# Token layout and early issue order of a fused attention and feed-forward kernel: 64 lanes of 7 tokens against 112 lanes of 4, with another order of the first twelve pairs

## The chip, the cores and the metric

The kernel runs on one core of a Trainium2 chip. The core has five engines, each with its own instruction stream that is executed in order: TensorE (PE, matrix products), VectorE (DVE), ScalarE (ACT), GpSimd (POOL) and SyncE (SP, which here only issues DMAs). Engines wait for each other and for DMAs through semaphores. The metric is the device time of one execution in microseconds (us), where less is better. Several runs are made and their median is compared.

## The reference

```python
# q, k, v: 8 x 12 heads x 448 tokens x 64
q_n, k_n = rmsnorm(q, g_q), rmsnorm(k, g_k)      # x / sqrt(mean(x*x) + 1e-6) * g
scores = q_n @ k_n.T / sqrt(64)
attn   = softmax(scores)                         # + 1e-9 under the sum
x      = (attn @ v), heads side by side          # 3584 tokens x 768
h      = x @ w_in                                # 768 x 2048
out    = (h * sigmoid(1.702 * h)) @ w_out        # 2048 x 768
```

Attention with a root-mean-square norm on q and k is followed by a gated feed-forward layer over all tokens.

## The kernel before

**Tiling.** The unit of attention is a *pair*: two heads of one batch element. There are 48 pairs, six to a batch element. The 448 tokens of a pair are laid out on the partitions of on-chip memory. In the kernel before, a partition holds seven consecutive tokens and 64 lanes hold one head's tokens; q sits on the even partitions and k on the odd ones, so that the two share a tile of 128 partitions. v is loaded twice over the same way, four tokens on the even partition of a lane and four on the odd one, with the middle token in both.

**One pair.** `load` (L541 to L555) brings q, k and v in. `square` (L557) and `reduce` (L564) form the sums of squares. For the first six pairs `by_log` (L577) turns them into 1/rms with a logarithm and an exponential on ACT; later pairs are taken three at a time by `seed` and `rsqrt`, on DVE and POOL. `norm` (L614) scales the rows, on POOL mostly. The rows are then transposed so that the head dimension lies on the partitions: for the first twelve pairs by PE (`turn_pe`, with the copies `take_q` and `take_k` on DVE), for the others by a transposing DMA (`turn_dma`, with `scale_k` on ACT and `part_k` on POOL). `score` (L692) multiplies q and k, `expo` (L713) takes the exponential on ACT, and `values` (L731) multiplies with v, where a column of ones gives the softmax sums. `divide` (L748) divides by these, and the result is turned back into `xt`, the input of the feed-forward layer. `vcast` (L622) casts v to bf16.

With seven tokens a lane, keys are handled in three full chunks of 128 per head (two tokens each) and one chunk in which the last token of both heads shares the 128 partitions. `gG2`, `of_head` and `v_of_head` are the masks which that shared chunk needs: in `both_heads` on the key side, in `vcast` on the value side.

**Feed-forward.** `first` (L960), `tanh` (L970), `gate` (L982), then a second product: plain (L990) for the first part, afterwards in a Strassen form with sums on DVE (L1035) and products (L1044). PE's work here runs over all 128 partitions. The weights come in as eight DMAs issued by POOL (four quarters of `w_in`, L927, and four of `w_out`, L933).

**Buffers.** There are rings of seven raw q/k buffers, seven raw v buffers, six buffers of transposed q and k, and six of cast v. In the first part of the program some members of each ring are pieces of one large tile named `late`, which the feed-forward layer uses later: two of the seven raw q/k buffers, three of the raw v buffers, three of the transposed buffers and four of the cast v. A line of the profile with `late` as its tile is thus a load, a transposed operand or a cast v, according to its source line.

**What sets the order.** Every step is a task of an order that is written out when the program is built (`_Order`). A list scheduler with a duration for each task, and a model of two DMA queues, picks at each engine the ready task with the lowest key. The queues are the hardware queue that SP (and once ACT) feeds and the software queue that POOL feeds. When both have work, `share` says which part of full speed each gets. Keys of the first sixteen or so pairs' tasks come from a table (`KEYS`), earliest issue times of their loads and of the weights from another (`AT`), and a third (`ON`) names the tasks that run on their second choice of engine. PE gets small filler products (L529) where the scheduler leaves it idle. The engines then run this fixed order; waits on semaphores are put in for every tile that one instruction writes and another touches.

Of the kernel before, what the change touches and what calls it, by code (L numbers as in the profile page):

```python
# [26 lines left out]
class _Order:  # L27
# [36 lines left out]
    def run(self):  # L64
# [32 lines left out]
        def share(t):  # L97
            n = len(heads())
            if n != 2:
                return 1.0 / n  # L100
            return 0.65 if not queues["sw"] else 0.55 if t.eng == "POOL" else 0.5
# [124 lines left out]
    'g': -7.96, 'gT': -29.21, 'gG': -3.44, ('S', 0, 0): 20.14, ('R', 0, 0): 28.16, ('S', 0, 1):  # L226
    44.18, ('R', 0, 1): -37.1, ('Q', 0): 43.05, ('N', 0, 0): 37.04, ('N', 0, 1): 35.09, ('V',
    0): -24.15, ('T', 0, 0): -33.92, ('T', 0, 1): 14.65, ('KQ', 0): 28.15, ('K', 0): 55.2, ('S',
    1, 0): 8.44, ('R', 1, 0): 20.3, ('S', 1, 1): 40.54, ('R', 1, 1): 21.55, ('Q', 1): -38.14,
    ('N', 1, 0): 10.45, ('N', 1, 1): -15.44, ('V', 1): 15.95, ('T', 1, 0): 28.13, ('T', 1, 1):  # L230
    -33.93, ('KQ', 1): 50.88, ('K', 1): 48.8, ('S', 2, 0): 38.84, ('R', 2, 0): 8.79, ('Q', 2):
    13.62, ('N', 2, 0): 48.85, ('N', 2, 1): -24.39, ('V', 2): 40.55, ('T', 2, 0): -22.79, ('T',
    2, 1): -32.33, ('KQ', 2): 50.42, ('K', 2): -39.99, ('S', 3, 0): -4.3, ('R', 3, 0): 1.95,
    ('Q', 3): -34.1, ('N', 3, 0): -21.09, ('N', 3, 1): -3.62, ('V', 3): -4.91, ('T', 3, 0):
    -39.99, ('T', 3, 1): -18.9, ('KQ', 3): 50.91, ('K', 3): 46.36, ('S', 4, 0): 13.62, ('R', 4,
    0): 18.86, ('Q', 4): 36.65, ('N', 4, 0): -27.4, ('N', 4, 1): -14.52, ('V', 4): 8.33, ('T',
    4, 0): 60, ('T', 4, 1): -30.45, ('KQ', 4): 44.45, ('K', 4): 59.33, ('S', 5, 0): 15.52, ('R',
    5, 0): 50.42, ('Q', 5): 40.97, ('N', 5, 0): 51.99, ('N', 5, 1): 13.48, ('V', 5): 1.94, ('T',
    5, 0): -18.61, ('T', 5, 1): -29.22, ('KQ', 5): 28.16, ('K', 5): 1.08, ('L', 6, 0): -40,
    ('L', 6, 1): 14.08, ('L', 6, 2): -20.34, ('S', 6, 0): 10.24, ('R', 6, 0): -40, ('N', 6, 0):  # L240
    20.31, ('N', 6, 1): -15.44, ('V', 6): 8.34, ('T', 6, 0): -29.45, ('T', 6, 1): 15.28, ('KQ',
    6): 30.06, ('K', 6): -4.76, ('L', 7, 0): -31.18, ('L', 7, 1): 4.22, ('L', 7, 2): 57.6, ('S',
    7, 0): 32.32, ('R', 7, 0): 1.93, ('N', 7, 0): -7.89, ('N', 7, 1): -36.91, ('V', 7): 60,
    ('T', 7, 0): 5.3, ('T', 7, 1): -22.33, ('KQ', 7): 51.98, ('K', 7): 15.39, ('L', 8, 0):
    -14.16, ('L', 8, 1): -40, ('L', 8, 2): -20.32, ('S', 8, 0): 11.41, ('R', 8, 0): 59.33,
    ('Q0', 8): 53.43, ('Q', 8): -25.28, ('N', 8, 0): -3.63, ('N', 8, 1): -27.25, ('V', 8):
    28.31, ('T', 8, 0): 14.16, ('T', 8, 1): -40, ('KQ', 8): 1.15, ('K', 8): -8.89, ('L', 9, 0):
    -39.86, ('L', 9, 1): -11.5, ('L', 9, 2): 4.21, ('S', 9, 0): -14.54, ('R', 9, 0): 51.98,
    ('N', 9, 0): 35.63, ('N', 9, 1): -0.84, ('V', 9): 18.85, ('T', 9, 0): -23.2, ('T', 9, 1):
    -38.52, ('KQ', 9): 4.12, ('K', 9): 8.56, ('L', 10, 0): 12.98, ('L', 10, 1): 4.05, ('L', 10,  # L250
    2): -17.2, ('S', 10, 0): 10.46, ('R', 10, 0): 55.21, ('N', 10, 0): -7.97, ('N', 10, 1):
    0.16, ('V', 10): -24.2, ('T', 10, 0): -4.6, ('T', 10, 1): 9.68, ('KQ', 10): 8.78, ('K', 10):
    -3.43, ('L', 11, 0): -39.84, ('L', 11, 1): -39.67, ('L', 11, 2): 4.36, ('S', 11, 0): 42.54,
    ('R', 11, 0): -4.42, ('Q0', 11): -10.06, ('Q', 11): -14.57, ('N', 11, 0): 54.8, ('N', 11,
    1): 46.7, ('V', 11): 32.33, ('T', 11, 0): -39.99, ('T', 11, 1): -25.77, ('KQ', 11): 20.9,
    ('K', 11): 50.35, ('C', 0, 0, 0): -3.33, ('E', 0, 0, 0): 36.27, ('C', 0, 0, 1): -39.06,
    ('E', 0, 0, 1): 42.1, ('P', 0, 0, 0, 0): -18.92, ('P', 0, 0, 0, 1): -7.65, ('P', 0, 0, 0,
    2): -18.93, ('P', 0, 0, 0, 3): -39.99, ('O', 0, 0, 0): -40, ('B', 0, 0): -29.68, ('X', 0,
    0): 45.25, ('C', 1, 0, 0): 19.37, ('E', 1, 0, 0): -13.6, ('C', 1, 0, 1): -39.96, ('E', 1, 0,
    1): 13.61, ('P', 1, 0, 0, 0): -22.78, ('P', 1, 0, 0, 1): -40, ('P', 1, 0, 0, 2): -35.63,  # L260
    ('P', 1, 0, 0, 3): -35.79, ('O', 1, 0, 0): 1.36, ('B', 1, 0): 31.62, ('X', 1, 0): 50.63,
    ('C', 2, 0, 0): -18.6, ('E', 2, 0, 0): 13.51, ('C', 2, 0, 1): -25.35, ('E', 2, 0, 1): 51.3,
    ('P', 2, 0, 0, 0): -32.5, ('P', 2, 0, 0, 1): -39.99, ('P', 2, 0, 0, 2): -37.82, ('P', 2, 0,
    0, 3): -34.28, ('O', 2, 0, 0): 50.48, ('B', 2, 0): -39.07, ('X', 2, 0): 2.32, ('C', 3, 0,
    0): -29.04, ('E', 3, 0, 0): 8.46, ('C', 3, 0, 1): -29.48, ('E', 3, 0, 1): -22.67, ('P', 3,
    0, 0, 0): -20.87, ('P', 3, 0, 0, 1): -18.58, ('P', 3, 0, 0, 2): 15.26, ('P', 3, 0, 0, 3):
    -29.36, ('O', 3, 0, 0): 28.64, ('B', 3, 0): -35.53, ('X', 3, 0): -33.23, ('C', 4, 0, 0):
    -33.94, ('E', 4, 0, 0): -38.12, ('C', 4, 0, 1): -39.99, ('E', 4, 0, 1): 57.75, ('P', 4, 0,
    0, 0): -11.24, ('P', 4, 0, 0, 1): -40, ('P', 4, 0, 0, 2): -28.01, ('P', 4, 0, 0, 3): 15.27,
    ('O', 4, 0, 0): 50.21, ('B', 4, 0): -30.29, ('X', 4, 0): 8.79, ('C', 5, 0, 0): -19.24, ('E',  # L270
    5, 0, 0): -37.99, ('C', 5, 0, 1): -33.93, ('E', 5, 0, 1): 15.32, ('P', 5, 0, 0, 0): -32.06,
    ('P', 5, 0, 0, 1): 13.53, ('P', 5, 0, 0, 2): -18.89, ('P', 5, 0, 0, 3): 31.63, ('O', 5, 0,
    0): -0.32, ('B', 5, 0): -34.64, ('X', 5, 0): -8.9, ('C', 0, 1, 0): -25.97, ('E', 0, 1, 0):
    1.69, ('C', 0, 1, 1): -16.66, ('E', 0, 1, 1): 42.54, ('P', 0, 1, 0, 0): 20.38, ('P', 0, 1,
    0, 1): -35.54, ('P', 0, 1, 0, 2): -34.27, ('P', 0, 1, 0, 3): 18.62, ('O', 0, 1, 0): -0.33,
    ('B', 0, 1): -40, ('X', 0, 1): 59.93, ('C', 1, 1, 0): -40, ('E', 1, 1, 0): 59.1, ('C', 1, 1,
    1): -23.35, ('E', 1, 1, 1): 59.09, ('P', 1, 1, 0, 0): 19.56, ('P', 1, 1, 0, 1): -33.42,
    ('P', 1, 1, 0, 2): -23.22, ('P', 1, 1, 0, 3): 13.53, ('O', 1, 1, 0): 50.91, ('B', 1, 1):
    -31.11, ('X', 1, 1): -1.55, ('C', 2, 1, 0): -0.85, ('E', 2, 1, 0): -39.35, ('C', 2, 1, 1):
    13.53, ('E', 2, 1, 1): 12.93, ('P', 2, 1, 0, 0): 15.4, ('P', 2, 1, 0, 1): -0.36, ('P', 2, 1,  # L280
    0, 2): -33.43, ('P', 2, 1, 0, 3): 5.29, ('O', 2, 1, 0): 53.15, ('B', 2, 1): -39.05, ('X', 2,
    1): 32.15, ('C', 3, 1, 0): -20.21, ('E', 3, 1, 0): -0.21, ('C', 3, 1, 1): -34.68, ('E', 3,
    1, 1): -38.13, ('P', 3, 1, 0, 0): -4.54, ('P', 3, 1, 0, 1): -36.55, ('P', 3, 1, 0, 2):
    -0.32, ('P', 3, 1, 0, 3): 31.62, ('O', 3, 1, 0): 27.76, ('B', 3, 1): -40, ('X', 3, 1):
    28.15, ('C', 4, 1, 0): 9.08, ('E', 4, 1, 0): 42.53, ('C', 4, 1, 1): 4.27, ('E', 4, 1, 1):
    42.1, ('P', 4, 1, 0, 0): -4.29, ('P', 4, 1, 0, 1): 9.68, ('P', 4, 1, 0, 2): 9.81, ('P', 4,
    1, 0, 3): -28.0, ('O', 4, 1, 0): 50.2, ('B', 4, 1): -18.93, ('X', 4, 1): 13.19, ('C', 5, 1,
    0): -39.98, ('E', 5, 1, 0): -22.76, ('C', 5, 1, 1): -29.55, ('E', 5, 1, 1): 15.51, ('P', 5,
    1, 0, 0): -23.19, ('P', 5, 1, 0, 1): 4.26, ('P', 5, 1, 0, 2): -18.93, ('P', 5, 1, 0, 3):
    -35.21, ('O', 5, 1, 0): 8.55, ('B', 5, 1): 9.83, ('X', 5, 1): -40, ('C', 6, None, 0):  # L290
    -25.14, ('E', 6, None, 0): -22.75, ('E', 6, None, 1): 51.16, ('C', 6, None, 2): -40, ('E',
    6, None, 2): 13.49, ('E', 6, None, 3): 10.84, ('P', 6, None, 0, 0): -38.03, ('P', 6, None,
    0, 1): -30.29, ('P', 6, None, 0, 2): 41.42, ('P', 6, None, 0, 3): -34.28, ('O', 6, None, 0):
    58.71, ('P', 6, None, 1, 0): 24.43, ('P', 6, None, 1, 1): 3.72, ('P', 6, None, 1, 2):
    -32.51, ('P', 6, None, 1, 3): 13.54, ('O', 6, None, 1): -40, ('B', 6, None): -35.8, ('X', 6,
    None): 50.9, ('C', 7, None, 0): 18.62, ('E', 7, None, 0): 41.4, ('E', 7, None, 1): 33.89,
    ('C', 7, None, 2): 7.37, ('E', 7, None, 2): 60, ('E', 7, None, 3): 48.79, ('P', 7, None, 0,
# [1006 lines left out]
```

## Time and profile before

| | us |
|---|---|
| median of three runs (476.58 to 479.13) | 478.04 |
| the profiled execution | 478.04 |
| its span, first to last instruction | 476.3 |
| PE busy | 421.2 (88% of the span) |
| DVE / ACT / POOL busy | 295.3 / 280.3 / 203.5 |

The span is cut into 40 slices of 11.9 us by the page's second part, and the profile's table of windows gives the same for any stretch. Read so, the kernel has two parts. From about 97 us on PE is busy nearly without a break (43.00 us of the 43.00 from 97 to 140, 49.95 us of the 50.00 from 140 to 190). Before that it is busy 53.3 us of 97, and part of these are fillers. A busy share is an average, so an engine with half its time idle in the first part still tells nothing by itself: the chain of waits and the table of who waited for whom say what each idle stretch waited for. SPq and POOLq stand for the sequencers that issue DMAs. The bar of a DMA in the timeline is its issue; its data lands later.

### The profile page before, as it was taken

To read this page: it belongs to the slowest core of one execution; us is meant where nothing else is said; L and a number is where in the kernel's file an instruction comes from. 1 tells how busy PE (TensorE), PEld (TensorE's weight loads), DVE (VectorE), ACT (ScalarE), POOL (GpSimd) and SP (SyncE) were. 2 spreads that over 40 slices of the span, in tenths; PEclk is the share of its full clock that TensorE was granted. 3 is DMA by queue.
4 is the path that set the end of the run, shared out by engine and by line. 5 is a ranking of instruction groups with operands and counts; after the bars stand their busy time and mean duration, and the time that the engine had idled before them with its cause. 6 is when DMAs were issued, how large, how long until landed. Compare 5 with 4: busy or idle time off the path is not lost.

```text
span 476.3 us, 9605 instructions
## 1 busy us (share of the span) xinstructions
PE 421.2 (88%) x3604; PEld 250.1 (53%) x3604; DVE 295.3 (62%) x600; ACT 280.3 (59%) x431; POOL 203.5 (43%) x322
## 2 busy tenths in 40 slices
PE   4833388399999999998899999999999999999996
PEld 2422267287665555554455565445555555555563
DVE  3732257569769778658557874577666655565573
ACT  2541166177869886778479754696777456722410
POOL 5543237372673847726363773266464312000000
PEclk9756579789999999999899999999999999999999
DMA  5956669496377587676578567865653453013014
GB/s 171 244 153 146 128 128 209 132 189 168 65 186 138 112 203 173 166 193 146 133 183 205 121 145 179 179 171 134 158 126 79 105 128 81 19 28 77 0 43 108
DMA packets 94642, 64.93 MB, mean 136 GB/s; under 512 B 55684, under 2 KB 94596, under 8 KB 94596
## 3 DMA queue, kind: packets, MB, share of 16 engines
q1 hardware_dynamic: 86992, 57.60, 49.3%
q0 software_dynamic: 7296, 6.29, 8.7%
q8 instruction: 28, 0.46, 0.4%
q10 hardware_dynamic: 308, 0.43, 0.3%
q14 instruction: 18, 0.15, 0.1%
HBM read 47.19 MB, written 11.01 MB: 122 GB/s over the span
## 4 chain that ended last, share of the span: by engine, by line
PE 71%; DMA 10%; DVE 6%; issue 4%; SPq 3%; POOL 2%; ACT 2%; POOLq 0%; DVEq 0%; ACTq 0%
PE w L960 24%; PE w L1044 18%; PE o L744 6%; PE sc L707 6%; DMA late<-in_v_dram 4%; PE sc L1044 4%; PE w L990 3%; DMA raw<-in_k_dram 3%; PE o L741 3%; PE sc L710 3%; PE sc L960 2%; DVE late L1035 2%; SPq L548 2%; POOL row L619 1%; DVE ssq L571 1%
## 5 line engine op out<-in xcount | busy, mean ns | idle before, releaser
L719 ACT ACTIVATE att<-sc 128x896 bf16<-128x896 f32 (+1 forms) x168 | 130.2, 825 | 54.6 <-PE sc L707 54.2
L960 PE MATMUL w<-xt,w_in_s 128*128 128x448 bf16 (+1 forms) x810 | 152.4, 333 | 1.8 <-DVE g L982 1.8
L960 PEld LDWEIGHTS <-w_in_s 128*128 128x128 bf16 x864 | 80.1, 99 | 51.7 <-issue 3.3
L982 DVE SCALAR_TENSOR_TENSOR g<-th,w 128x448 bf16<-128x448 f32 x119 | 72.3, 616 | 26.4 <-ACT th L970 26.2
L970 ACT ACTIVATE th<-w 128x448 f32<-128x448 f32 x119 | 64.4, 548 | 34.3 <-PE w L960 32.0
L619 POOL TENSOR_TENSOR row<-raw,rs 128x384 bf16<-128x384 f32 (+1 forms) x85 | 84.2, 1011 | 0.9 <-issue 0.5
L626 POOL TENSOR_TENSOR vx<-vraw,v_of_head 128x512 bf16<-128x512 f32 x36 | 38.8, 1079 | 84.1 <-PE o L744 49.3
L744 PEld LDWEIGHTS <-att 128*128 128x128 bf16 x1152 | 63.7, 101 | 18.9 <-issue 2.8
L571 DVE TENSOR_REDUCE ssq<-sq 128x14 f32<-128x896 f32 (+1 forms) x50 | 51.9, 1043 | 27.0 <-ACT sq L562 26.2
L744 PE MATMUL o<-vx,att 128*128 128x65 bf16 x960 | 65.6, 196 | 0.0
L562 ACT ACTIVATE sq<-raw 128x896 f32<-128x896 f32 (+1 forms) x40 | 37.2, 933 | 23.8 <-DMA raw<-in_k_dram 13.4
L753 DVE RECIPROCAL rcp<-o 112x4 f32<-112x4 f32 x96 | 17.1, 178 | 48.7 <-PE o L744 48.4
L754 DVE TENSOR_TENSOR obs<-o,rcp 112x256 bf16<-112x256 f32 x96 | 40.8, 424 | 3.3
L707 PE MATMUL sc<-qk 64*128 64x448 bf16 (+1 forms) x270 | 41.7, 363 | 0.2 <-ACT att L719 0.2
L1044 PEld LDWEIGHTS <-late 128*128 128x128 bf16 x344 | 31.0, 98 | 19.9 <-issue 2.6
L741 PEld LDWEIGHTS <-att 128*128 128x128 bf16 x192 | 19.2, 100 | 41.8 <-issue 12.3
L1044 PEld LDWEIGHTS <-g 128*128 128x128 bf16 x336 | 30.4, 99 | 17.8 <-issue 1.5
L741 PE MATMUL o<-vx,att 128*128 128x130 bf16 x160 | 36.2, 226 | 4.0 <-DVE obs L754 3.3
L1044 PE MATMUL w<-w_out_s,g 128*128 128x384 bf16 x176 | 34.9, 335 | 0.0
L1044 PE MATMUL w<-w_out_s,late 128*128 128x384 bf16 x152 | 29.7, 326 | 0.3 <-DVE late L1035 0.2
L1044 PE MATMUL w<-late 128*128 128x384 bf16 x152 | 29.8, 327 | 0.0
L1057 DVE TENSOR_SCALAR osb<-w 128x384 f32<-128x384 f32 x29 | 16.2, 557 | 21.8 <-PE w L1044 21.7
(106 smaller groups left out, 469.7 us busy)
## 6 DMA issues: line engine op xcount, KB each, us to landing
vraw<-in_v_dram SPq DMA_DIRECT2D x84, 128.0 KB, 2.8
raw<-in_q_dram SPq DMA_DIRECT2D x44, 224.0 KB, 3.5
raw<-in_k_dram SPq DMA_DIRECT2D x43, 224.0 KB, 3.4
out_dram<-osb SPq DMA_DIRECT2D x88, 96.0 KB, 2.2
w_in_s<-in_moe_w_in_dram POOLq DMA_DIRECT2D x4, 768.0 KB, 9.6
w_out_s<-in_moe_w_out_dram POOLq DMA_DIRECT2D x4, 768.0 KB, 13.8
out_dram<-att SPq DMA_DIRECT2D x22, 96.0 KB, 2.2
late<-in_v_dram SPq DMA_DIRECT2D x12, 128.0 KB, 7.0
```

The source lines that it names most:

```text
L571: nc.vector.reduce_sum(out=ssq_of[g0][:, i - g0, part], in_=sq[i % N_SQ][:, part], axis=AX.X)
L619: eng.tensor_tensor(out=row_ring[i % N_QKN][:, gi:NT:2].rearrange("p n (h d) -> p h n d", h=2), in0=raw[turn(i, N_RAW, K_RAW)][:, :, ns], ...
L626: eng.tensor_tensor(out=vx_ring[turn(i, N_V, K_V)][:, :, :D], in0=vraw[turn(i, N_RAW, K_VRAW)][:, :, :], in1=v_of_head[:, :].to_broadcast( ...
L707: nc.tensor.matmul(sc[:, hp, lo:lo + n], lhsT=ks[r, c * WIN:(c + 1) * WIN], rhs=qs[r], start=True, stop=True)
L719: nc.scalar.activation(out=o, in_=sc[:, :, :S] if t < NC else sc[:, 0, :S], func=ACT.Exp)
L741: nc.tensor.matmul(o[:, x:x + 2, :], lhsT=att_of(u)[:, NT - 2, qs * SS:qs * SS + WIN], rhs=vx[:, NC:NC + 2, :], start=True, stop=True)
L744: nc.tensor.matmul(o[:, x, :], lhsT=att_of(u)[:, at, qs * SS:qs * SS + WIN], rhs=vx[:, (NC + 2) * hp + c, :], start=False, stop=(c == NC - 1),
L754: nc.vector.tensor_tensor(out=to[:SS, 2 * w:2 * w + 2].rearrange("p n h d -> p (n h) d"), in0=o[:SS, :, :D], in1=rcp[:SS, :].to_broadcast( ...
L960: nc.tensor.matmul(gps[b, m][:, j * SH:j * SH + n], lhsT=w_in_s[:, ki, f * 128:(f + 1) * 128], rhs=xT[b][:, ki, lo:lo + n], start=(ki == 0 ...
L970: nc.scalar.activation(out=th[:, :], in_=gps[b, m][:, :S], func=ACT.Tanh, scale=0.851)
L982: nc.vector.scalar_tensor_tensor(out=g_of[b // 2][:, f:f + len(g), lo:lo + n], in0=view(ths.pop((b, m))[:, :]), scalar=1.0, in1=view(gps.p ...
L1044: nc.tensor.matmul(held[to], lhsT=lhs[:, ko, :], rhs=y[:, ko, :], start=first and ko == 0, stop=ko == NK - 1, skip_group_check=not first)
```

## The change

The layout of tokens becomes 112 lanes of 4, with q and k side by side in the free dimension instead of on alternate partitions. A chunk of keys is then 112 tokens of one head, four chunks per head, and the shared chunk goes with its masks. v is loaded once, by one DMA. In the early transposes and the DMA transposes there are eight blocks of 112 in place of seven of 128. For the later pairs q is scaled by the gains instead of k, by one ACT instruction without the POOL one. Output rows are stored in pieces of up to 112 rows. On the side of the order, the shares in the scheduler's DMA model, the tables `KEYS`, `AT` and `ON` and the durations of many tasks are other ones. The number of PE's fillers is 78 in place of 77.

```diff
-            return 0.65 if not queues["sw"] else 0.55 if t.eng == "POOL" else 0.5
+            return 0.65 if not queues["sw"] else 0.69 if t.eng == "POOL" else 0.47
 KEYS = {
...
 AT = {
...
-    1): 12820, ('WI', 2): 4055, ('WI', 3): 32041, ('WO', 0): 27995, ('WO', 1): 6438, ('WO', 2):
-    20685, ('WO', 3): 53587}
+    15, 0): 18221, ('L', 15, 1): 27573, ('L', 15, 2): 45426, ('WI', 0): 11048, ('WI', 1): 3173,
+    ('WI', 2): 27789, ('WI', 3): 20304, ('WO', 0): 14524, ('WO', 1): 53302, ('WO', 2): 44189,
+    ('WO', 3): 21000}
...
-    late = consts.tile([128, 3 * T_LEN + N_SUM * S_LEN + 1056], BF16, name="late", tag="late")
+    late = consts.tile([128, 3 * T_LEN + N_SUM * S_LEN], BF16, name="late", tag="late")
...
-        src = (q, k, v)[which][b, h0:h0 + 2].rearrange("h (s n) d -> s h (n d)", n=NT)
+        src = (q, k, v)[which][b, h0:h0 + 2].rearrange("h (ss ns) d -> ss h ns d", ns=NS)
         if which == 2:
-            four = (NC + 1) * D
-            for side in range(2):
-                nc.sync.dma_start(
-                    out=vraw[turn(i, N_RAW, K_VRAW)][side::2].rearrange("p (h n) d -> p h (n d)", h=2),
-                    in_=bass.AP(tensor=src.tensor, offset=src.offset + side * four,
-                                ap=[[NT * D, LN], [S * D - D, 2], [1, four]]))
+            nc.sync.dma_start(out=vraw[turn(i, N_RAW, K_VRAW)][:SS], in_=src)
             return
         eng = nc.scalar if i == 0 and which == 1 else nc.sync
-        eng.dma_start(out=raw[turn(i, N_RAW, K_RAW)][which::2].rearrange("p h n d -> p h (n d)"),
-                      in_=src)
+        eng.dma_start(out=raw[turn(i, N_RAW, K_RAW)][:SS, which], in_=src)
...
-        nc.vector.tensor_scalar(
-            out=parts_of(i)[1].rearrange("p (c s e) -> p c e s", c=NC, e=2),
-            in0=lanes(x[:, :2 * NC * WIN])[:, 1], scalar1=gG[:, :], scalar2=None, op0=ALU.mult)
-        both_heads(i, nc.vector, x)
+        nc.vector.tensor_scalar(out=qk_ring[turn(i, N_KZ, K_KZ)][:, 1], in0=tps[i][:, 1],
+                                scalar1=gG[:, :], scalar2=None, op0=ALU.mult)
...
-    def scale_k(i):
-        nc.scalar.activation(out=parts_of(i)[1].rearrange("p (c s e) -> p c e s", c=NC, e=2),
-                             in_=lanes(turned(i)[:, :2 * NC * WIN])[:, 1], func=ACT.Identity,
-                             scale=gG[:, :])
-    def part_k(i):
-        both_heads(i, nc.gpsimd, turned(i))
+    def scale_q(i):
+        t = qk_ring[turn(i, N_KZ, K_KZ)][:, 0]
+        nc.scalar.activation(out=t, in_=t, func=ACT.Identity, scale=gG[:, :])
...
-        keys = [2 * c + hp for c in range(NC - 1)] + [NT - 3 + 2 * hp]
-        if hp == 0:
-            nc.tensor.matmul(o[:, x:x + 2, :], lhsT=att_of(u)[:, NT - 2, qs * SS:qs * SS + WIN],
-                             rhs=vx[:, NC:NC + 2, :], start=True, stop=True)
-        for c, at in enumerate(keys):
-            nc.tensor.matmul(o[:, x, :], lhsT=att_of(u)[:, at, qs * SS:qs * SS + WIN],
-                             rhs=vx[:, (NC + 2) * hp + c, :], start=False, stop=(c == NC - 1),
-                             skip_group_check=True)
+        for kc in range(NS):
+            nc.tensor.matmul(os_[u, w][:, x, :],
+                             lhsT=att_of(u)[:SS, kc, hp, qs * SS:qs * SS + WIN],
+                             rhs=vx_ring[turn(i, N_V, K_V)][:SS, hp, kc, :],
+                             start=(kc == 0), stop=(kc == NS - 1))
...
-            od.add(("KB", i), "POOL", 400, lambda i=i: part_k(i), at - 1.5,
-                   deps=[("T", i, 1), "gG"] + kz_free)
-            od.add(("KQ", i), "ACT", 625, lambda i=i: scale_k(i), at - 1.5,
+            od.add(("KQ", i), "ACT", 662, lambda i=i: scale_q(i), at - 1.5,
                    deps=[("T", i, 1), ("gG")])
...
-        for c in range(tm * 128, (tm + 1) * 128, LN):
-            b, n = 2 * bp + c // S, token_at[c % S // LN]
+        while c < (tm + 1) * 128:
+            b, j = 2 * bp + c // S, c % S
+            ns, ss = j // SS, j % SS
+            n = min(SS - ss, (tm + 1) * 128 - c)
```

## The prediction

> **What bounds the kernel now.** I first read the page's slices: the share of PE's time, the clock granted to it, and the DMA engines.
>
> ```profile
> PE   4833388399999999998899999999999999999996
> ...
> PEclk9756579789999999999899999999999999999999
> ...
> DMA  5956669496377587676578567865653453013014
> ```
>
> From the ninth slice on PE is full and its clock is up. Before that five slices show 3 or 4. The windows give the amounts (columns: start to end, length, then busy time of PE, PEld, DVE, ACT and POOL, each with its count, then the clock, the DMA share and GB/s):
>
> ```profile
> 14.00:97.00 83.00, 46.54 (x471) 32.34 (x471) 38.43 (x83) 32.37 (x48) 36.37 (x40) 0.71 0.71 158
> ...
> 140.00:190.00 50.00, 49.95 (x451) 28.25 (x450) 42.27 (x82) 41.06 (x64) 28.41 (x43) 1.00 0.73 160
> ```
>
> In the first no engine is even 60% busy, so something makes them all wait. The second is PE-bound; DVE (85%) and ACT (82%) come closest behind. PE's table of waits up to 97 us, its largest rows (total, times, longest):
>
> ```profile
> PE o L741 <- DMA late<-in_v_dram: 13.3, 3, 8.1
> PE w L637 <- POOL row L619: 9.0, 2, 8.1
> PE sc L707 <- DMA late<-in_v_dram: 7.9, 1, 7.9
> ...
> PE o L741 <- DMA late<-in_k_dram: 2.7, 1, 2.7
> PE sc L707 <- DMA late<-in_q_dram: 1.5, 1, 1.5
> ```
>
> These products read transposed q and k or cast v, yet wait for loads of raw tokens. The chain of waits (start, us, what) has the same loads on it:
>
> ```profile
> 20.89 7.59 DMA raw<-in_k_dram
> ...
> 39.18 7.03 DMA late<-in_v_dram
> ...
> 51.43 7.32 DMA late<-in_v_dram
> ```
>
> And this is the timeline of the second one, with all engines standing:
>
> ```profile
> 37.70 0.89 POOL L927 DMA_DIRECT2D w_in_s<-in_moe_w_in_dram  x1
> 38.52 1.25 SPq L548 DMA_DIRECT2D late<-in_v_dram  x2
> ...
> 46.30 0.69 DVE L626 TENSOR_TENSOR late<-late,v_of_head 128x512 bf16<-128x512 f32 x1 [7.92 <-DMA late<-in_v_dram]
> 46.34 0.56 PE L707 MATMUL sc<-late 64*128 64x224 bf16 x4 [7.89 <-DMA late<-in_v_dram]
> 46.37 2.15 POOL L560 TENSOR_TENSOR sq<-late 128x896 f32<-128x896 f32 x1 [7.79 <-DMA late<-in_v_dram]
> ```
>
> A load of v issued just after a quarter of `w_in` takes 7.0 us, where page part 6 has a median of 2.8 us for such loads. PE's scores and POOL's squares don't use its data and stand still all the same. The listing of the built programs, with each instruction's semaphores, says why: before, this product waits for two semaphores of v loads into `late`, and the earlier one on row 308 of PE for six DMAs. `late` is one tile with many pieces, and the waits treat a write on every second partition as touching all of it (why exactly is my reading). In the changed program PE's list has no wait for a load queue's semaphore up to its first operand from a transposing DMA, far into the full-PE part; ACT, DVE and POOL wait only for the loads that they read.
>
> **What the Trainium skill says.** "DMA: Bandwidth & Descriptors", section "Queues, rings and completion order": each DMA engine takes turns between queues, but drains a whole packet of descriptors (up to 64) before it switches. The trace agrees in kind: part 3 has 7296 packets on the software queue for eight weight loads, 912 each or 57 per engine, and a load behind one waited some 4 us longer than alone. The same page under "Why a DMA increments its semaphore by 16 and not by 1": the engines used are the largest number up to 16 that divides the outer dimension on both sides. 64 and 112 lanes and all new store pieces (16 to 112 rows) are multiples of 16, so no load falls to fewer engines; no run here shows it for 112. "TensorE: Matmul & The Clock Gate", "What's actually happening": an idle window of about 3.4 us drops PE's clock to half. The clock of 0.71 from 14 to 97 us agrees.
>
> **The change part by part**, against the profiled execution (span 476.3 us and 1.7 us around it, 478.04, which is also the median).
>
> 1. *Start.* SP's first load, which writes `late`, waited for POOL's memsets till 3.56 us; ACT issues its own load at 0.75. In the changed order SP's first load goes to `raw` and has no wait: 3.56 − 0.75 = 2.8 us less. Either end: 0 if the gains' load (read at 11.05) is what comes late, 3.5 at most. I take −2.8.
>
> 2. *False waits gone.* On PE: 13.3 + 7.9 + 2.7 + 1.5, and 8.1 of the row wait (ending 30.6), whose POOL instruction stood behind a cast into `late` waiting for the load of 20.89: together 33.5 us. On the chain: 7.59 + 7.03 + 7.32 and, further on, 2.94, 2.28, 2.87 and 3.57, 33.6 us. I take −33.5. The cover they gave goes too: loads and weights moved meanwhile.
>
> 3. *Weights come in clumps.* The changed POOL order has two quarters of `w_in` back to back behind its first square and two half norms, near 12 us (here the first norms end at 13 to 17), the other two behind a norm of pair 5, one of `w_out` a square later, and three of `w_out` together later. The software queue takes 8.7% of 476.3 us of all DMA engines, 41.4 us for eight, so 5.2 us each. The first clump holds the queue 10.4 us while loads of pairs 3 to 5 are still due (17 loads at SP's 0.605 us each take till 11 or 12 us to issue). These are true waits. They are covered in part by the attention of pairs 0 to 2; DVE and ACT stand behind them in order. From 0 to 10; I take +5. The second clump (15.6 us) meets the loads of pairs 7 and 8, whose sums of squares stand on DVE ahead of the first gates: 0 to 10, I take +4.
>
> 4. *DMA as a floor.* A pair was 224 + 224 + 256 KB; it becomes 3 x 224. At the second slice's 244 GB/s that is 3.0 and 2.8 us. Twelve pairs and eight weights: 34 + 41 = 75 us in place of 77. The second product needs its first `w_out` at 115 us now; 20 us earlier still leaves 95. No cost, but little slack.
>
> 5. *More vector work.* Squares, sums and norms go over 1024 elements in place of 896, on 112 partitions. Sum: 1080 x 1024/896 = 1.23 us, +0.15 on DVE for 48 pairs. Without stalls DVE has 38.4 + 2 us to do in some 60: +2.
>
> 6. *Late pairs on ACT.* Four exponentials of 896 in place of three and one of 448: 917 − 548 = +0.37. Square: 952 x 1024/896 = 1088, +0.14. Scaling 448 elements in one run instead of 384 in pieces (733): between −0.15 and +0.12, I take 0. So +0.5 us for 36 pairs, 18 us of ACT. PE covers it: in the densest window some six pairs add 3 us to ACT's 41 of 50 (and 1 to DVE's 42). Where cover fails, chains from load to exponential get longer; 0 to 12, I take +3. POOL loses `part_k` (0.45) and gains 0.2 on norms.
>
> 7. *PE.* `values` has 32 products of 65 columns in place of 28, four of which had 130. In the timeline the groups start 151.09, 151.34 and 151.59: 0.25 us for 7 with 520 columns, as many as in the new 8. If columns set it, nothing; if instructions, 1/7 more: 0.036 x 4 x 48 = 6.9 us. The product of 130 takes 0.06, the next six 0.19, so two of 65 against one of 130 are 0.063 to 0.060: 0.003 x 4 x 48 = 0.6. Transposes: one more in each of twelve pairs, 12 x 0.08 = 1.0. Scores: two rows of paired products take 0.5 us for 4, the shared chunk 0.22 alone: equal. +1.5.
>
> 8. *SP* issues three loads a pair for four; each has 224 rows for 128, so 0.6 to 1.06 us: −0.6 to +0.8 a pair, hidden since SP waits for buffers. Stores are as many as before. 0.
>
> Sum: −2.8 − 33.5 + 5 + 4 + 2 + 3 + 1.5 = −20.8, which gives 457.2 us.
>
> **The rivals.**
>
> *More is won.* Clumps hide behind work and the clock stays up: −36.3 + 1.5 and half of 5 and 6 (+2.5) is −32, 446; with a warm clock 440. For it: PE has only 46.5 us to do from 14 to 97, fillers included. Against: DMA share is 0.71 already.
>
> *Half is lost again.* True waits for clumped weights take 20 us in place of 9: 468.
>
> *Slower: starvation for the length of every clump.* A load behind one weight load took 7.0 to 7.6 us. At 7.3 each, clumps of two, three and three are 15, 22 and 22 us. If all engines stand in order behind a starved load each time, 59 us come in for 36 that go: 478 − 36 + 59 + 6 = 507; from about 30 us of it on, half, the kernel is slower. For: the engines' orders are fixed, and this trace shows what one late load does. Against: raw buffers for seven pairs are filled ahead, and in the changed program a late load stops only its readers.
>
> *It doesn't do what it says.* The named waits go from the listing, but the loads were due there anyway: same, 478. Against: the products that stood here at 39 and 51 us wait for no load in the changed listing.
>
> **How the numbers follow.** Forecast (448 to 466) 0.55; more won 0.17; half lost 0.12; same 0.05; slower 0.11. A measurement here can tell 0.5%, 2.4 us, from no change. Faster: 0.84; same 0.05; slower 0.11. The likeliest is 457. Down to 438 and up to 476 leaves out about 0.05 below and 0.14 above.
>
> **What would show it.** Right: PE's waits for `late<-in_` gone; first tanh (71.1 us now) near 50 to 55; first plain second product (114.9) near 95; first full slice two slices earlier; ACT near 44 of 50 us in dense windows. Wrong: waits of 5 us or more of ACT, DVE and POOL on `raw<-in_` loads near 15 to 25 and 30 to 45 us, or PE idle of more than 15 us after the start-up, behind ACT.

## The result, and the profile after

The changed kernel takes 426.24 us (median, 424.02 to 429.03) where the kernel before, run beside it on the same chip, takes 478.12. The ratio is 0.892 with a 95% interval of 0.886 to 0.898. It is faster by 52 us; the forecast was 21, and its range ended at 438. All times here and below are medians of runs in the faster of the chip's two states; one run of e4 (512.3 us), which fell in the slower one, is left out.

The slices of the page, after (40 slices of 10.6 us):

```profile
PE   5998899999999999999999999999999999999995
...
PEclk9899999999999999999999999999999999999999
...
DMA  9999999768379987667548688556334630120023
```

The hole of the first eight slices is gone. PE is at 8 or 9 from the second slice on, its clock stays up, and the DMA engines are full for the first seven slices, where before five of the first seven stood at 5 or 6 tenths. The windows for the two stretches that the prediction showed (columns as there), after:

```profile
14.00:97.00 83.00, 77.48 (x1003) 55.38 (x999) 61.52 (x138) 68.69 (x96) 56.74 (x75) 1.00 1.05 225
140.00:190.00 50.00, 49.12 (x451) 27.09 (x449) 38.10 (x72) 42.00 (x61) 29.22 (x46) 1.00 0.77 189
```

PE does 77.5 us of work from 14 to 97 us in place of 46.5. The dense part is as full as it was. PE's table of waits up to 97 us, after, its largest rows:

```profile
PE w L618 <- DVE row L595: 2.2, 2, 1.3
PE w L894 <- DVE xt L713: 1.7, 1, 1.7
PE w L894 <- DVE g L916: 1.5, 1, 1.5
```

No row of that table is a wait for a load, into `late` or elsewhere, and the longest single wait is 1.7 us where it was 8.1.

To see where the time came from, I cut both executions at one milestone that both have: the first plain second product (L990 before, L924 after), at 114.9 us before and 69.1 us after. The windows on both sides of it, before:

```profile
0.00:114.90 114.90, 71.17 (x711) 52.25 (x712) 58.25 (x130) 49.84 (x77) 53.31 (x83) 0.76 0.74 169
114.90:476.30 361.40, 349.99 (x2895) 197.88 (x2893) 237.08 (x472) 230.49 (x354) 150.17 (x239) 0.99 0.54 126
```

and after:

```profile
0.00:69.10 69.10, 58.64 (x760) 45.37 (x761) 51.54 (x114) 50.52 (x75) 49.00 (x78) 0.98 1.14 242
69.10:425.70 356.60, 349.25 (x3108) 195.26 (x3104) 242.00 (x470) 249.33 (x360) 142.88 (x203) 1.00 0.55 131
```

Length less PE's busy time is PE's idle time. So the milestone came 45.8 us sooner: 33.3 us of idle time went (43.7 to 10.5), and 12.5 us of busy time (71.2 to 58.6), although PE issued 49 products more. Nearly the same work lies ahead of the milestone in both: 192 products of `first`, 32 groups of products of `values`, and the transposes of 11 pairs before, 10.5 after. The rest of the program became 4.8 us shorter, 4.1 of it idle time. The sum, 50.6, is the difference of the two spans.

### The profile page after: what moved, and what is told of

Read it like the earlier page. It is cut to its first block, busy times and chain, and to the rows that moved or that the text cites. A ratio compares the mean times of both kernels' runs of the same rounds, so it can differ in the third digit from the quotient of the medians.

```text
span 425.7 us, 10013 instructions
## 1 busy us (share of the span) xinstructions
PE 407.9 (96%) x3863; PEld 240.6 (57%) x3863; DVE 293.5 (69%) x583; ACT 299.9 (70%) x434; POOL 191.9 (45%) x281
## 4 chain that ended last, share of the span: by engine, by line
PE 77%; DVE 10%; DMA 9%; issue 2%; ACT 2%; POOL 0%; SPq 0%; DVEq 0%; ACTq 0%
PE w L894 29%; PE w L984 18%; PE o L683 10%; PE sc L662 8%; PE sc L984 4%; DMA vraw<-in_v_dram 4%; DMA raw<-in_q_dram 4%; PE w L924 3%; DVE late L975 3%; PE sc L894 2%; DVE ssq L553 2%; DVE obs L694 1%; DMA raw<-in_k_dram 1%; DVE late L964 1%; PE w L618 1%
## 5 line engine op out<-in xcount | busy, mean ns | idle before, releaser
L670 ACT ACTIVATE att<-sc 112x896 bf16<-112x896 f32 x168 | 146.0, 918 | 32.0 <-PE sc L662 31.7
L683 PEld LDWEIGHTS <-att 112*128 112x128 bf16 x1536 | 73.3, 98 | 46.6 <-issue 15.3
L595 POOL TENSOR_TENSOR row<-raw,rs 112x512 bf16<-112x512 f32 x82 | 88.4, 1103 | 18.3 <-DMA qk<-row 15.2
L608 POOL TENSOR_TENSOR vx<-vraw,ones 112x512 bf16<-112x512 f32 x35 | 37.2, 1062 | 89.3 <-PE o L683 57.4
L683 PE MATMUL o<-vx,att 112*128 112x65 bf16 x1280 | 74.5, 194 | 2.8 <-DVE obs L694 2.7
L553 DVE TENSOR_REDUCE ssq<-sq 112x16 f32<-112x1024 f32 (+1 forms) x50 | 58.4, 1171 | 14.5 <-ACT sq L544 12.4
L544 ACT ACTIVATE sq<-raw 112x1024 f32<-112x1024 f32 (+1 forms) x41 | 42.0, 1029 | 14.6 <-DMA raw<-in_k_dram 7.9
L662 PE MATMUL sc<-qk 64*128 64x448 bf16 (+1 forms) x360 | 47.6, 344 | 0.1
L585 POOL TENSOR_TENSOR t<-rs 112x48 f32<-112x48 f32 x28 | 7.5, 267 | 44.1 <-DVE rs L574 40.0
L636 ACT ACTIVATE qk<-qk,gG 128x448 bf16<-128x448 bf16 x36 | 24.2, 675 | 0.4 <-DMA qk<-row 0.4
## 6 DMA issues: line engine op xcount, KB each, us to landing
w_in_s<-in_moe_w_in_dram POOLq DMA_DIRECT2D x4, 768.0 KB, 16.2
```

Of the source, the lines that this page charges most:

```text
L544: nc.scalar.activation(out=sq[i % N_SQ][:SS, part], in_=raw[turn(i, N_RAW, K_RAW)][:SS, part], func=ACT.Square)
L553: nc.vector.reduce_sum(out=ssq_of[g0][:SS, i - g0, part], in_=sq[i % N_SQ][:SS, part], axis=AX.X)
L595: eng.tensor_tensor(out=row_ring[i % N_QKN][:SS, gi].rearrange("p n (h d) -> p h n d", h=2), in0=raw[turn(i, N_RAW, K_RAW)][:SS, gi], in1= ...
L608: nc.gpsimd.tensor_tensor(out=vx[:, :, :D], in0=vr, in1=ones[:SS, :].to_broadcast([SS, 2 * NS, D]), op=ALU.mult)
L662: nc.tensor.matmul(sc[:, hp, j * SH:j * SH + n], lhsT=qkw[r, k0:k0 + WIN], rhs=qk[r, 0, qs], start=True, stop=True)
L670: nc.scalar.activation(out=att[:SS, t, :, :S], in_=sc, func=ACT.Exp)
```

## The experiments

Theory A: waits of one piece of `late` for loads into another piece cost most of the time, and the cold clock of PE follows from them. Theory B: the new order of loads, weights and vector work won most of it. Later, theory C: an order that was searched for, as these tables were by my reading, fits only its own layout.

### The waits alone: taken from the kernel before, given to the changed one

The first kernel is the kernel before with one thing changed: where its early loads land. All engines' instructions and their order stay. One thing comes with it: SP's first load no longer waits for the memsets of `late`, and starts at 0.73 us in place of 3.56.

```diff
-    early_raw = [piece(2 * NT * D, FP32).rearrange(...) for _ in range(2)]
-    early_vraw = [piece((NT + 1) * D, FP32).rearrange(...) for _ in range(3)]
+    apart_t = [consts.tile([128, T_LEN], BF16, ...) for j in range(2)]   # later T2, T3
+    apart_s = [consts.tile([128, S_LEN], BF16, ...) for j in range(2)]   # later two sums
+    apart_o = consts.tile([128, 2 * HALF], FP32, ...)                    # later two of osb
+    early_raw = [views of apart_t]; early_vraw = [views of apart_s and apart_o]
```

> The kernel before, same order of all instructions; only the two early raw buffers and the three early v buffers are tiles of their own (their space is shared with the late terms and sums, and with two output buffers) instead of pieces of the tile late. Theory A (waits of one tile for another piece's loads cost most of the time, and the cold clock of PE is their consequence): 430 to 445 us, PE's waits on late<-in_ loads gone, clock from 14 to 97 us up from 0.71 to 0.9 or more. Theory B (the new order of loads, weights and vector work won most of it): 462 to 475 us, because the loads still come when they came.

Measured: 438.06 us, ratio 0.914 (0.908 to 0.920). Theory A holds. Its windows, cut at the same milestone (L993 in this kernel, at 74.36 us):

```profile
0.00:74.36 74.36, 62.97 (x712) 47.59 (x713) 56.85 (x130) 49.11 (x77) 52.22 (x83) 0.95 1.09 258
74.36:436.50 362.14, 348.40 (x2893) 197.07 (x2893) 236.48 (x471) 230.69 (x354) 151.45 (x239) 1.00 0.55 126
```

This is the cleanest comparison of the study. Against the first window of the kernel before, the counts say that the same work was done: 712 and 711 products, 130 DVE, 77 ACT and 83 POOL instructions. It took 40.5 us less. PE's idle time fell from 43.7 to 11.4 us, by 32.3. Its busy time fell from 71.2 to 63.0 us, by 8.2, with the clock at 0.95 in place of 0.76: the same products, run warmer. After the milestone next to nothing was given back (362.1 us to 361.4).

The second kernel goes the other way: the changed kernel, with each load into an early piece of `late` split into even and odd partitions. The third is its control, with the same loads split into two whole halves.

```diff
+        for part in [slice(0, SS, 2), slice(1, SS, 2)] if at >= 0 else [slice(0, SS)]:   # e2
+        for part in [slice(0, SS // 2), slice(SS // 2, SS)] if at >= 0 else [slice(0, SS)]:   # e3
+            eng.dma_start(out=to[part], in_=src[part])
```

> The changed kernel, with each load into an early buffer inside late issued as two, even partitions and odd partitions, so that it writes every second partition as the kernel before did. The bytes and the order are the same. Theory A: the waits come back on PE, 450 to 470 us. Theory B: 427 to 434 us, only what two loads cost in place of one.

> Control for the stepped one: the same loads in two halves of 56 whole neighbouring partitions. Both theories: 426 to 432 us; what it is above the changed kernel is the price of the second load.

Measured: 475.17 us stepped (ratio 0.991, 0.989 to 0.994) and 428.19 us in halves (0.894, 0.887 to 0.901). The stepped writes cost 47 us against their control, somewhat more than expected; the second load costs 2 by the medians, not clear of noise. PE's waits up to 97 us in the stepped kernel:

```profile
PE o L685 <- DMA late<-in_v_dram: 13.7, 3, 6.3
PE w L620 <- DVE late L624: 13.3, 1, 13.3
PE o L685 <- DMA late<-in_k_dram: 6.7, 2, 3.8
PE o L685 <- DMA late<-in_q_dram: 5.5, 1, 5.5
```

Products that read cast v wait again for loads of raw q, k and v. The second row is the same thing at one remove: DVE itself stood for 12.7 us in its cast into `late` (L607) until a load of q. In the listing of the built program, PE's first score that reads a piece of `late` waits for all eight of the hardware queue's semaphores; in halves, in the changed kernel and in e1, PE waits for none of them before its first operand from a transposing DMA. The window from 14 to 97 us of the stepped kernel has 41.8 us of PE work at a clock of 0.68, close to the 46.5 us at 0.71 of the kernel before.

### The order alone: tables changed without the layout

Four kernels cross the layouts with the tables `KEYS`, `AT` and `ON` and the two shares.

```diff
 # e4: the kernel before;   e6, e12: the kernel before with its early loads apart (e1)
+KEYS, AT, ON, shares 0.69 / 0.47 of the changed kernel
 # e5: the changed kernel
+KEYS, AT, ON, shares 0.55 / 0.5 of the kernel before
 # e7: the changed kernel
-            ... 0.69 if t.eng == "POOL" else 0.47
+            ... 0.55 if t.eng == "POOL" else 0.5
```

> The kernel before (64 lanes of 7, loads on every second partition) with the priorities, earliest times, engine choices and queue shares of the changed kernel. Theory A: 465 to 490 us, since the layout makes the waits whatever the order. Theory B: 440 to 455 us.

> The layout of the changed kernel (112 lanes of 4) with the priorities, earliest times, engine choices and queue shares of the kernel before. Theory A (the layout's waits were nearly all): 426 to 436 us. Theory C (priorities fit only the layout that they were searched for, so they are worth more than 10 us here): 440 to 465 us, with PE idle in the first 100 us for true reasons, its producers late.

> The kernel before with its early loads in tiles of their own (no waits on other pieces' loads) and the tables and shares of the changed kernel. If those tables are better whatever the layout: 425 to 432 us. Theory C: 440 to 465 us, above the same kernel with its own tables (438).

> As e6_apart_newtables, but the two output buffers that share space with an early v buffer are given out only when that buffer's last cast is done (in e6 they were taken too soon, and pair 13's v was overwritten). Expected 458 to 464 us, as e6, since only the late part of the first slice is touched; under 450 us if the conflict itself cost the time.

> The changed kernel with the two constants of the DMA queues' shares back at 0.55 and 0.5. Only the planned ends of transfers move, and with them the order in the early part. If the shares matter by themselves: 432 to 445 us. If the priorities carry the order: 425 to 431 us.

Measured, in this order: e4 505.72 us (ratio 1.062, 1.052 to 1.073), e5 447.46 (0.936, 0.932 to 0.940), e6 461.73 (0.966, 0.961 to 0.972), e12 465.22 (0.974, 0.970 to 0.977, a little above what was expected) and e7 427.51 (0.894, 0.889 to 0.899). e6 leaves out a wait, so that an output overwrites v of pair 13; e12 has the wait and is the one that counts.

The new tables make the kernel before slower by 26 us, more than either theory had said. They make it slower by 27 also where its waits are gone (465.2 against 438.1), so this is not the waits. The old tables cost the changed layout 21. The shares are worth nothing that can be told from zero. For these two layouts theory C holds and theory B does not. Part of where the old tables hurt shows in e5's window from 97 to 140 us, where the changed kernel has 42.89 us of PE work at a clock of 1.00, and in e5's PE waits from 85 to 200 us:

```profile
97.00:140.00 43.00, 36.30 (x335) 18.75 (x333) 31.01 (x59) 35.36 (x51) 23.38 (x35) 0.84 0.52 124
```

```profile
PE o L683 <- DVE obs L694: 4.6, 6, 1.3
PE o L683 <- ACT att L670: 2.2, 3, 1.0
```

PE waits inside the attention chain. These are true waits: for the exponential, whose result the products read, and for the division, which has to read the products' output `o` before they write it again. The clock falls to 0.84 with them.

That raised the question of what the tables are worth at all. Two kernels have no tables at all, only the default keys, times and engines, and the same shares.

```diff
 # e13: the kernel before with its early loads apart;   e14: the changed kernel
+KEYS = {}
+AT = {}
+ON = set()
```

> The kernel before with its early loads in tiles of their own, and no table at all: default priorities, earliest times and engines, shares 0.55 and 0.5. If the searched order matters much on either layout: 450 to 475 us, 12 to 37 above the same kernel with its tables (438).

> The changed kernel with no table at all, the same defaults and the same shares 0.55 and 0.5. Against e13 this is the layout alone, with neither side's waits nor searched order: if the 12 us between the separated kernel before (438) and the changed one (426) come from the layout, 8 to 16 us less than e13; if they come from a better find of the search, within 4 us of e13.

Measured: 438.40 us (ratio 0.914, 0.909 to 0.920) and 429.72 (0.895, 0.890 to 0.901). The first is the time of the same kernel with its tables (438.06), so the expectation of 450 and more was missed. The second is 3.5 us above the changed kernel, and the two intervals overlap. Between the two layouts, with no waits on pieces and no searched order on either side, lie 8.7 us. The profiled executions lie 11.4 us apart, since that of e14 was its fastest. The first part of their pages, e13 ahead of e14:

```profile
PE 411.7 (94%) x3605; PEld 245.0 (56%) x3605; DVE 290.9 (67%) x599; ACT 283.9 (65%) x438; POOL 193.3 (44%) x316
```

```profile
PE 408.5 (96%) x3859; PEld 240.9 (57%) x3859; DVE 290.5 (68%) x577; ACT 305.2 (72%) x441; POOL 190.1 (45%) x280
```

PE issues 254 products more and is busy 3 us less; the other 8 us are idle time (436.9 - 411.7 = 25.2 and 425.5 - 408.5 = 17.0). So the 52 us are, one after the other: some 40 the waits between pieces, with the clock and the start; some 9 the layout without them; and 3.5 by the medians, not clear of noise, the order.

### The prediction's terms: start, clumps, ACT

Each of these leaves the order of the changed kernel's other instructions as it is, except for e8, where the weights' new times make the scheduler plan anew.

```diff
 # e8: AT without its eight weights (default times: 12, 16.5, 21, 25.5 and 38, 45, 52, 59 us)
 # e11: on POOL alone, one weight of each w_in clump and two of the w_out clump held back
+HOLD = {("WI", 1): 3, ("WI", 3): 1, ("WO", 2): 2, ("WO", 3): 4}   # by so many POOL tasks
 # e9: SP's first load waits for POOL's last memset
+    nc.gpsimd.memset(raw[0][:, 0, 0, 0, :8], 0.0)
 # e10: in scale_q, once more
+        nc.scalar.activation(out=t, in_=t, func=ACT.Identity, scale=ones[:, :])
```

> The changed kernel with the eight weight loads at evenly spaced earliest times (12, 16.5, 21, 25.5 and 38, 45, 52, 59 us) in place of clumps. By step 3 of the prediction the clumps cost up to 9 us, so 417 to 424 us. By the rival that loads lie far enough ahead of their readers: 424 to 432 us, no better.

> The changed kernel with nothing moved but POOL's weight loads: the second of each pair of w_in and the second and third of the clump of w_out stand one to three tasks later on POOL, with other work between. Step 3 of the prediction (clumps cost 9 us): 417 to 423 us. Rival (what the clumps delay lies far enough ahead of its readers): 425 to 428 us. If late weights stop PE instead: over 429 us.

> The changed kernel; one small memset on POOL, behind its other memsets, writes the buffer of SP's first load, so that all of SP's loads start some 2.8 us later, as in the kernel before. Step 1 of the prediction: 429 us, 2.8 more than the changed kernel. Rival, the start is hidden by what comes late anyway (the gains, the first norms): 426 to 427 us.

> The changed kernel; the scaling of transposed q on ACT in each of the 36 late pairs is followed by a second one with the factor 1, 0.67 us each, 24 us of ACT in all, order otherwise the same. At the rate of step 6 of the prediction (3 us for 18 us of ACT): 430 us. If PE covers ACT's added work wholly: 426 to 427.5 us. If ACT is close to being the bound in those pairs: 436 us or more.

Measured: e8 450.37 us (ratio 0.941, 0.937 to 0.944), e11 427.65 (0.895, 0.892 to 0.898), e9 428.07 (0.897, 0.894 to 0.901), e10 429.21 (0.898, 0.895 to 0.901).

With the clumps pulled apart and nothing else moved (e11), the time is that of the changed kernel, so the clumping costs nothing that can be told from zero. It does not show what late loads cost: with both queues full the loads stayed as slow in e11, where the two longest on its chain of waits took 14.9 and 14.6 us. e8 was slower by 24 us, which neither expectation had. It changes the planned order on all engines, so it says nothing of clumps on the chip; it fits theory C, since a table with part of its entries gone is 21 us worse than no table, but what in that order costs the time I did not follow up. A late start (e9, where SP's first load begins at 2.68 us in place of 0.74) costs 1.8 us, and 20 us more of ACT's busy time (e10; 299.9 to 319.9) cost 3.0 by the medians. The intervals of both touch that of the changed kernel (0.886 to 0.898), and against e11, which was run beside them, they are 0.4 and 1.6. So neither cost can be told from nothing.

## Why the prediction was wrong

The waits on `late` were read rightly. The price of everything else was not, and the kernel landed below even the rival *More is won* (440 with a warm clock). The spans of three profiled executions split the miss: 476.3 us before, 436.5 with the early loads apart (e1), 425.7 after.

**Steps 1 and 2, start and false waits: right.** They had −36.3 us, and e1, which has both and nothing else, gives −39.8. That they are so near is luck, since two misses nearly cancel: 32.3 us of idle time went before the milestone, less than forecast, and 8.2 us of busy time, which the sum had at nothing. PE's clock from 14 to 97 us, 0.71, was read in that very profile, yet its cost stood only in the rival *More is won*, for 6 us there. e2 brought the waits back from the other side, and e2 against its control, e3, shows the reading of the stepped writes: a load on every second partition of one piece makes readers of other pieces wait.

The idle stretches and the clock go together as "TensorE: Matmul & The Clock Gate", section "What's actually happening", has it, which the prediction cites: with the waits apart the longest wait of PE up to 97 us is 2.3 us, where it was 8.1, and the clock from 14 to 97 is 0.98. e5 does not fit a rule of single idle stretches of some 3.4 us: there the clock fell to 0.50 after shorter waits (last section).

One reading of the lines was off. The median of 2.8 us, with which the prediction compares its load of 7.0, is that of loads of v into `vraw`; for the twelve into `late` the same part of the page has 7.0. "Some 4 us longer than alone" is thus not shown. The wait itself is.

**The step that failed is the price of the layout and the order, steps 3, 5, 6 and 7: +15.5 us in the sum, −10.8 in the runs.** From e1 to the changed kernel 5.3 us went before the milestone and 5.5 after it. That is 26.3 us of the 29.8 by which the forecast missed the profiled execution (457.2 for 427.4); the waits with their clock are the other 3.5. Term by term:

**Step 3, weights in clumps: the loads were starved, their readers hardly.** I took +9 and got nothing that can be told from zero (e11, for the clumping). The chain of waits of the changed kernel has what I feared (columns: start, us, what):

```profile
14.40 12.89 DMA vraw<-in_v_dram
27.31 15.43 DMA raw<-in_q_dram
42.85 1.06 ACT sq L544
```

These loads took 13 and 15 us, longer than the 7 us in the kernel before that cost so much. But little stands behind them. ACT waited 3.6 us for the second, no engine waited longer for a load from 14 to 50 us, and PE, with no wait for a load at all, had 31.2 us to do in these 36. I had written that argument under the rival *Slower*, and then still took 9 of a possible 20 into the sum.

**Step 5, more vector work: one side left out.** I counted the longer sums of squares (1080 to 1214 ns, near the forecast) and left out the copies after PE's transposes, which the diff shows. Groups of DVE by form, before (x6 is one half of the twelve pairs):

```profile
L653 DVE TENSOR_SCALAR qk<-w,gG 128x384 bf16<-128x384 bf16 x6 | 3.9, 642 | 0.0
L649 DVE COPY qk<-w 128x448 bf16<-128x448 bf16 x6 | 3.6, 620 | 0.8 <-PE w L637 0.8
L659 DVE TENSOR_TENSOR qk<-w,gG 128x128 bf16<-128x128 bf16 x6 | 1.7, 276 | 0.0
```

and after:

```profile
L625 DVE TENSOR_SCALAR qk<-w,gG 128x448 bf16<-128x448 bf16 x6 | 2.6, 446 | 0.2
L622 DVE COPY qk<-w 128x448 bf16<-128x448 bf16 x6 | 2.2, 381 | 0.4 <-PE w L618 0.4
```

642 + 620 + 276 ns became 446 + 381, 0.71 us less for each of twelve pairs, 8.5 us in all. Up to the milestone DVE had 51.5 us to do in place of 58.3 (56.9 in e1). So DVE's work in the early part fell where the step had it rise. What that won in time was not tested alone.

**Steps 6 and 7, late pairs: the work as forecast, the time not.** ACT's busy time rose by 19.6 us (18 forecast), and e10 puts the price of that much at 3.0 us or less by the medians. PE's busy time fell from e1 to the changed kernel, 411.4 to 407.9 us, where step 7 had +1.5. And the part after the milestone became 5.5 us shorter than in e1. The two kernels without tables say the same of the layout alone: from e13 to e14 PE loses 8.2 us of idle time, and 6.2 of it (15.6 to 9.4) lie after 110 us, when the last early transpose was long done (66 and 68 us). So at least 6.2 of the 11.4 us between these two spans are not the early copies of step 5. In e13 PE waits 3.8 us for the gate (`g`, from DVE) after 140 us, in e14 not at all; what in the layout does this stays open.

**Step 4, DMA: right that it costs nothing, with a floor that was too high.** I had put the first second product near 95 us and the floor for twelve pairs and all weights near 75. It came at 69.1. By then the loads of 18 pairs and all eight weights had been issued, and all but 1.1 of the weights' 6.3 MB had landed. The floor took 5.2 us for a weight, which is 151 GB/s, beside 244 GB/s for the pairs; the DMA engines moved 242 GB/s over the whole 69.1 us, and at that rate twelve pairs and eight weights are an estimated 60 us. Step 8, SP, showed no cost: the issue of a load into `raw` took 0.35 to 0.43 us by the medians up to 70 us, less than the 0.6 to 1.06 that was allowed.

Of the signs named beforehand, the waits on `late<-in_` went as said, and the signs of being wrong did not come: the longest wait of ACT, DVE or POOL for a load from 14 to 50 us is 3.6 us. ACT reached 42.0 us of the 50 from 140 to 190, not 44. The early signs came far sooner than forecast: first tanh at 36.0 us for 50 to 55, first second product at 69.1 for 95, first full slice seven slices earlier for two.

## What to carry to other kernels

A wait for data that an instruction does not read is visible in two places: in the table of waits, as a product waiting for a raw load, and in the built program's semaphores. If buffers share a tile, look at which shapes of writes go into it; giving the loads tiles of their own won some 40 of these 52 us with no change to any engine's order. When idle time of PE is priced, price the clock with it: here each 4 us of idle time that went took 1 us of busy time along (32.3 and 8.2). And costs that a change adds are to be priced beside the work that it takes away: here that was the larger error. Last, tables that set an order are no property of the program alone: with the other layout's tables both layouts were 18 to 27 us slower than with none, and with their own 0 to 3.5 us faster, which is within the noise.

## What the runs showed of the hardware that was not expected

With both DMA queues kept full, the core's DMA engines moved 248 GB/s from 14 to 50 us at a counted share of 1.18, so the share by this count can pass 1 and is no ceiling; the kernel before moved 158 GB/s at 0.71 from 14 to 97 us. In that state a quarter of `w_in` needed 16.2 us from issue to landing by the median, and loads of q and k into `raw` in the first 60 us some 10 us, where over the whole program they need 4.1 and 4.7. Pulling the weights apart did not shorten the longest loads (e11, 14.9 us), and PE's table of waits up to 97 us has none of them.

The granted clock can fall without one long wait of PE. In e5 it read 0.50 from 106 to 118 us, though PE's longest wait from 97 to 140 us was 1.3 us. What preceded it was thin work: PE was busy 1.77 us of the 3.4 up to 105.8. The clock came back after some 4 us in which PE was busy without a break (115 to 119 us). Whether the busy share of such a stretch is what counts was not tested.
